# A fused mixer and two feed-forward layers on one core: the opening stretch of the instruction stream put in order by a list scheduler, and two more units' decays made by products

## The chip, the cores and the metric

One core of one Trainium2 chip. The metric is the device time of one execution in microseconds; the median of 3 runs of the kernel before is 615.81 us (613.55 to 616.11).

## The reference

A chunked linear attention with decays, then two feed-forward layers over its output. Inputs x (4 batches, 8 heads, 768 steps, 32 wide), decays a, and B, C (16 states) are 32-bit floats; the weights come as 64-bit floats.

```python
for c in range(nc):                      # chunks of 32 steps
    cum = np.cumsum(la, axis=-1)         # la: log of the decays
    L = np.exp(cum[:, :, :, None] - cum[:, :, None, :]) * causal
    M = np.einsum('bhin,bhjn->bhij', Cc, Bc) * L
    y[:, :, sl] = M @ xc + (Cc @ state) * np.exp(cum)[..., None]
    state = decay_full * state + sum_j(Bc_j * xc_j * decay_from_j)
x = y as (3072 tokens, 256)
h = (x @ w1) * (x @ w2)                  # 256 -> 1024
x2 = (h @ w3) @ w_out                    # 1024 -> 1024 -> 256
h2 = np.maximum(x2 @ w_in, 0.0)          # 256 -> 2048
out = (h2 * h2) @ w_out2                 # 2048 -> 256
```

## The kernel before

The kernel multiplies w3 by w_out once (`wc`, from 16 steps `wc_step` of 8 products each in the trace), so that h @ w3 @ w_out becomes one product with a 1024 x 256 matrix. Every feed-forward product is made three times with operands split in a high and a low part (`mm3`, L99 to L102).

**Weights.** 44 pieces of 128 x 512 double words (0.52 MB each) come through SP's DMA queue into 7 raw buffers (4 `rawe`, 3 `rawl`; `load_next`, L178, issues at L193). A piece is decoded from 64 to 32 bits in `decode1` (ACT L206 and POOL L208, one on each half of a double word) and `decode2` (DVE L221, which joins the halves). The 24 pieces of w1, w2, w_in (`wi`) and the last weight (`wo`) are then split in `decode3` (ACT L231 makes the high part, POOL L232 the low part). The pieces of w3 and the first w_out (`wo1`) go unsplit into `wc`.

**Units.** The attention is cut into 16 units (a batch's half of the sequence, 4 heads, 4 chunks of 96). A unit scans its decays (`u_decay`, DVE L272), weighs B with them (`u_bd`, POOL L287 and L294), makes B times C and the state's gains on PE (`u_cb`, L350; `u_gain`, L305), multiplies the decays in (`u_m`, L363), steps and carries the state (`u_state`, `u_carry`), and multiplies out (`u_y`, L370; `u_x`, `u_xl`). The decays of units 0 and 1 come to the scan by a product of PE that copies a row to all partitions in PSUM (`u_rows`, L259); those of units 2 to 15 are written to DRAM and read back, broadcast to 112 partitions (`load_la`, L139).

**Blocks.** The 3072 tokens go through the feed-forward layers in 7 blocks, 3 of 384 and 4 of 480. A block has 8 steps `ff_a` (products with w1 and w2), each followed by `ff_x2` with wc, and 16 steps `ff_h1`, `ff_h2` and `ff_o`: for 384 tokens 336 products.

**Order.** The order of the instructions of each engine is the order of this program; nothing reorders it. Ahead of block 0 are 29 slots (`n_first`): each runs parts of the decoding of one to three pieces, the `wc_step` that has become possible, and what the tables `first_steps` and `pre` give for units 0 and 1. Then each block has 24 slots, one per step; unit 2 begins 2 slots ahead of block 0, the others at the slots of `BEGIN`, with their 12 parts at the offsets of `unit_steps`. Unit 4 begins at slot 17 of block 0 and ends in block 1. The decoding of wi and wo goes on inside block 0.

The lines that set it:

```python
BEGIN = [None, None, -2, 8, 17, 26, 34, 42, 50, 57, 69, 79, 93, 103, 112, 122]
...
    for i in range(n_first):
        for f in pre.get(i, ()):
            f()
        if i >= LATE:
            decode(first=False)
        for key in [key for key in stage if key[0] == "w3"]:
            wc_step(key[1] % 2, key[1] // 2)
        run_fill()
        for _ in range(1 + (i == 0)):
            decode(second=False)
```

Of the kernel before, what the change touches and what calls it, by code (L numbers as in the profile page):

```python
# [15 lines left out]
T = 96  # L16
# [27 lines left out]
FIRST = 2  # L44
FSTEPS = 8


BEGIN = [None, None, -2, 8, 17, 26, 34, 42, 50, 57, 69, 79, 93, 103, 112, 122]
LATE = 1
# [3 lines left out]
def mixer_kernel(ctx, tc, a, bct, xb, cst, *rest):  # L53
# [61 lines left out]
    def clip_decays():  # L115
# [15 lines left out]
        for i in (0, 32):  # L131
            nc.vector.tensor_copy(sel[i:i + 32, :], cs[i:i + 32, i:i + H])
        z = az.rearrange("(b f g) (h i) -> f b (g h) i", f=2, g=2, i=LH)
        for f in range(2):
            nc.sync.dma_start(out=z[f], in_=t[:, f, :])

    def load_la(u, q):
        t = at.tile([TA, LA], F32, tag="la", name="la")
        q.dma_start(out=t, in_=az[u:u + 1, :].to_broadcast([TA, LA]))  # L139
        raw.setdefault(u, {})["la"] = t  # L140

    def load_bx(u, q):
        t = at.tile([TA, HC * D + HC * N], F32, tag="xa", name="xa")
        q.dma_start(out=t[0:T, :], in_=xb[u])
        for h in range(HG):
            src = bct[u, 0:64, :].rearrange("(n h) (c i) -> h n c i", h=HG, i=T)[h]
            q.dma_start(out=bt[u % 2][32 * h:32 * h + N, :, 0:T], in_=src)
        raw.setdefault(u, {})["xa"] = t

    def load_c(u, q):  # L150
        t = at.tile([128, TB], F32, tag="ct", name="ct", bufs=1)
        for h in range(HG):
            q.dma_start(out=t[32 * h:32 * h + N, :], in_=bct[u, 64:128, :].rearrange("(n h) i -> h n i", h=HG)[h])
        raw.setdefault(u, {})["ct"] = t
# [23 lines left out]
    def load_next():  # L178

        if not loads:  # L180
            return
        key = loads[0]
        for where, n in [("early", NRE)] * (key not in LAST) + [("late", NRL)]:
            if len(held.setdefault(where, [])) < n:
                break
        else:
            return
        loads.pop(0)
        i = min(i for i in range(n) if i not in held[where])
        held[where].append(i)  # L190
        t = (rawe if where == "early" else rawl)[:, i]
        dst = t.rearrange("p (k m) t -> p k (m t)", m=DM) if key[0] in ("wo1", "wo") else t
        nc.sync.dma_start(out=dst, in_=piece_src(key))  # L193
        words[key] = t, where, i
# [8 lines left out]
    def decode1(key):  # L203
        t = words[key][0]
        z = t[:, :, 1].bitcast(F32)
        nc.scalar.activation(z, z, AF.Prelu, scale=2.0 ** -112, alpha=2.0 ** 32)  # L206
        if True:
            nc.gpsimd.tensor_scalar(t[:, :, 0], t[:, :, 0], 0.876 * 2.0 ** -29, 0.49, ALU.mult, ALU.add)  # L208
        else:
            nc.scalar.activation(t[:, :, 0], t[:, :, 0], AF.Copy, bias=0.49, scale=0.876 * 2.0 ** -29)  # L210

    def decode2(key):
        t, where, i = words.pop(key)
        held[where].remove(i)
# [9 lines left out]
    def decode3(key):  # L224
        if key[0] in ("w3", "wo1"):
            return
        if key in (("wo", 0), ("wo", 4)):
            to_wo(key[1] // 4)
        hi, lo = split_to(key)
        v = stage.pop(key).bitcast(F32)  # L230
        nc.scalar.copy(hi, v)  # L231
        nc.gpsimd.tensor_tensor(lo, v, f32(hi), op=ALU.subtract)  # L232

    pend = []
    whole = []

    def decode(first=True, second=True):

        while second and whole:
            decode3(whole.pop(0))  # L240
        if second and pend:
            whole.append(pend.pop(0))
            decode2(whole[-1])
            load_next()
            load_next()
        if first and todo:
            decode1(todo[0])
            pend.append(todo.pop(0))
# [5 lines left out]
    def u_rows(u, h):  # L254

        if h == 0:
            un[u] = dict(raw[u], la=at.tile([TA, LA], F32, tag="la", name="la"))
        r = u % 2 * HG + h
        nc.tensor.matmul(  # L259
            rows[h % 2][0:TA, 0:LH],  # L260
            lhsT=sel[:, r:r + 1].to_broadcast([64, TA]),
            rhs=raw["a"][:, u // 2 % 2, :],
            start=True, stop=True,
        )

# [30 lines left out]
    def u_gain(u):  # L296
# [3 lines left out]
        if "yu" not in d:  # L300
            d["yu"] = ps_yu.tile([128, 512], F32, tag="yu", name="yu")
# [32 lines left out]
    def u_cb(u, hs):  # L334
# [3 lines left out]
        d["ct"] = raw[u]["ct"]  # L338
        for h in hs:
            if h < 2 or len(hs) == 2:  # L340
                d["cb", h] = ps_cb.tile([128, TB], F32, tag="cb", name="cb")
            elif h == 2:
                d["cb", h] = ps_w.tile([128, 512], F32, tag="w", name="cbw")[:, 0:TB]
            else:
                d["yu"] = ps_yu.tile([128, 512], F32, tag="yu", name="yu")
                d["cb", h] = d["yu"][:, 0:TB]
# [9 lines left out]
        if hs[-1] == HG - 1 and u + 1 < NU:  # L356
            load_c(u + 1, nc.sync)
# [36 lines left out]
    def u_xl(u):  # L394
        for lo, src, hi in un.pop(u)["x"]:
            nc.vector.tensor_tensor(lo, src, f32(hi), op=ALU.subtract)

    def u_next(u):

        raw.pop(u)  # L400
        if u + 2 < NU:
            if u + 2 >= FIRST:
                load_la(u + 2, nc.sync)
            load_bx(u + 2, nc.sync)

    def unit_steps(u):
# [42 lines left out]
    def ff_a(f, m):  # L449
        x, n = xt[f], FBS[f]  # L450
        ps = []
        for w in w12:
            p = ps_w.tile([128, 512], F32, tag="w", name="pw")[:, 0:n]
            for k in range(KD):
                mm3(p, [t[:, k, m * 128:(m + 1) * 128] for t in w], [t[:, k, 0:n] for t in x], k == 0, k == KD - 1)
            ps.append(p)
        asb = sb.tile([128, FB], F32, tag="s1", name="asb")[:, 0:n]
        nc.scalar.copy(asb, ps[0])  # L458
        pr = sb.tile([128, FB], F32, tag="s2", name="pr")[:, 0:n]
        nc.vector.tensor_tensor(pr, ps[1], asb, op=ALU.mult)  # L460
        pt[f, m] = [t[:, 0:n] for t in pair("s3", LAG + 1)]
        nc.scalar.copy(pt[f, m][0], pr)  # L462
        return lambda: nc.vector.tensor_tensor(pt[f, m][1], pr, f32(pt[f, m][0]), op=ALU.subtract)  # L463

    def ff_x2(f, m, e):
# [3 lines left out]
        if m == M1 - 1:  # L469
            if e == 0:  # L470
                x2[f] = [t[:, :, 0:FBS[f]] for t in pair("x2", 1, (128, KD, FB))]
            nc.scalar.copy(x2[f][0][:, e, :], acc["x2"][e])  # L472
            nc.vector.tensor_tensor(x2[f][1][:, e, :], acc["x2"][e], f32(x2[f][0][:, e, :]), op=ALU.subtract)
# [7 lines left out]
    def ff_h2(f, m):  # L481
        r = sb.tile([128, FB], F32, tag="s1", name="r")[:, 0:FBS[f]]
        nc.scalar.activation(r, hp.pop(m), AF.Relu)  # L483
        q = sb.tile([128, FB], F32, tag="s2", name="q")[:, 0:FBS[f]]

        (nc.gpsimd if f > 0 else nc.vector).tensor_tensor(q, r, r, op=ALU.mult)  # L486
        qt[f, m] = [t[:, 0:FBS[f]] for t in pair("s3", LAG + 1)]
        nc.scalar.activation(qt[f, m][0], r, AF.Square)  # L488
# [229 lines left out]
```

## Time and profile before

| | us |
|---|---|
| median of 3 runs | 615.81 |
| the profiled execution | 615.05 |
| its span | 613.3 |
| PE, DVE, ACT, POOL busy | 572.3, 317.2, 265.2, 213.4 |

The span runs from the first to the last instruction of the execution; the other 1.8 us lie around it. Busy shares are means over a stretch of opening work and seven blocks, so they are read stage by stage. A group of instructions has its line of the program, engine, operation, output and inputs, and count; in the prediction, L and a number is such a line.

### The profile page before, as it was taken

To read this page: it belongs to the slowest core of one execution; us is meant where nothing else is said; L and a number is where in the kernel's file an instruction comes from. 1 tells how busy PE (TensorE), PEld (TensorE's weight loads), DVE (VectorE), ACT (ScalarE), POOL (GpSimd) and SP (SyncE) were. 2 spreads that over 40 slices of the span, in tenths; PEclk is the share of its full clock that TensorE was granted. 3 is DMA by queue.
4 is the path that set the end of the run, shared out by engine and by line. 5 is a ranking of instruction groups with operands and counts; after the bars stand their busy time and mean duration, and the time that the engine had idled before them with its cause. 6 is when DMAs were issued, how large, how long until landed. Compare 5 with 4: busy or idle time off the path is not lost.

```text
span 613.3 us, 10509 instructions
## 1 busy us (share of the span) xinstructions
PE 572.3 (93%) x4036; PEld 497.6 (81%) x4036; DVE 317.2 (52%) x548; ACT 265.2 (43%) x524; POOL 213.4 (35%) x263
## 2 busy tenths in 40 slices
PE   4986869777999999999999999999999999999997
PEld 2754759566999999998988888888888888888886
DVE  4573565779474765565534635366636352232421
ACT  2334355546344553364323543335434254432543
POOL 3443678675103640153200732107330143300432
PEclk7888798989999999999999999999999999999999
DMA  7997752260211221211210220102110000000000
GB/s 214 301 264 252 272 171 77 92 192 0 79 63 42 77 75 35 73 53 33 73 33 1 79 71 1 40 2 76 49 35 32 1 1 1 1 34 0 1 0 33
DMA packets 20969, 44.86 MB, mean 73 GB/s; under 512 B 7592, under 2 KB 10648, under 8 KB 20920
## 3 DMA queue, kind: packets, MB, share of 16 engines
q1 hardware_dynamic: 20712, 43.93, 23.4%
q8 instruction: 32, 0.52, 0.4%
q10 hardware_dynamic: 208, 0.27, 0.2%
q14 instruction: 17, 0.14, 0.1%
HBM read 40.94 MB, written 3.25 MB: 72 GB/s over the span
## 4 chain that ended last, share of the span: by engine, by line
PE 82%; DVE 5%; POOL 5%; issue 3%; DMA 3%; ACT 1%; ACTq 0%; DVEq 0%; POOLq 0%; SPq 0%
PE pw L102 41%; PE acc L102 31%; PE acc L524 4%; PE yu L370 2%; PE cb L350 2%; DMA cs<-in_cst 1%; DVE la L272 1%; POOL w2l L232 1%; DMA rawe<-in_w3t 1%; PE yu L305 1%; DMA rawl<-in_wo 1%; POOL rawe L208 1%; POOL w1l L232 1%; DVE q L486 1%; DVE s3l L489 1%
## 5 line engine op out<-in xcount | busy, mean ns | idle before, releaser
L486 POOL TENSOR_TENSOR q<-r 128x480 f32<-128x480 f32 (+1 forms) x96 | 103.0, 1076 | 227.0 <-ACT r L483 193.4
L489 DVE TENSOR_TENSOR s3l<-q,s3h 128x480 fp32r<-128x480 f32 (+1 forms) x112 | 74.4, 668 | 116.6 <-POOL q L486 115.5
L102 PE MATMUL acc<-s3h,wo 128*128 128x480 f32 (+1 forms) x448 | 128.5, 368 | 0.0
L483 ACT ACTIVATE r<-pw 128x480 f32<-128x480 f32 (+1 forms) x112 | 59.9, 535 | 120.4 <-PE pw L102 110.7
L102 PEld LDWEIGHTS acc<-s3h,wo 128*128 128x128 f32 x448 | 82.8, 190 | 9.4 <-issue 0.3
L102 PE MATMUL pw<-x2h,wih 128*128 128x480 f32 (+1 forms) x224 | 83.1, 371 | 1.5 <-ACT r L483 0.8
L102 PE MATMUL acc<-s3l,wo 128*128 128x480 f32 (+1 forms) x224 | 82.0, 366 | 2.2 <-DVE s3l L489 2.2
L102 PE MATMUL pw<-x2h,wil 128*128 128x480 f32 (+1 forms) x224 | 81.4, 363 | 0.0
L102 PE MATMUL pw<-x2l,wih 128*128 128x480 f32 (+1 forms) x224 | 79.2, 364 | 0.0
L460 DVE TENSOR_TENSOR pr<-pw,asb 128x480 f32<-128x480 f32 (+1 forms) x56 | 34.4, 614 | 85.3 <-PE pw L102 83.5
L488 ACT ACTIVATE s3h<-r 128x480 fp32r<-128x480 f32 (+1 forms) x112 | 64.0, 571 | 3.5
L462 ACT CAST s3h<-pr 128x480 fp32r<-128x480 f32 (+1 forms) x56 | 31.3, 559 | 78.3 <-DVE pr L460 78.3
L272 DVE TENSOR_TENSOR_SCAN la<-la,cs 112x384 f32<-112x384 f32 x56 | 63.7, 1137 | 0.0
L458 ACT COPY asb<-pw 128x480 f32<-128x480 f32 (+1 forms) x56 | 29.3, 523 | 58.4 <-PE pw L102 58.0
L287 POOL TENSOR_TENSOR bd<-xa,la 96x256 f32<-96x256 f32 x16 | 12.7, 796 | 109.9 <-DVE la L286 47.2
L102 PEld LDWEIGHTS pw<-x2h,wih 128*128 128x128 f32 x224 | 42.4, 189 | 8.9 <-ACT x2h L472 2.7
L524 PE MATMUL acc<-wo1v,ve 128*128 128x256 f32 x128 | 39.1, 469 | 10.5 <-DVE ve L221 10.4
L102 PEld LDWEIGHTS acc<-s3l,wo 128*128 128x128 f32 x224 | 42.5, 190 | 6.9 <-DVE s3l L489 3.1
L102 PEld LDWEIGHTS pw<-x2h,wil 128*128 128x128 f32 x224 | 42.4, 189 | 3.8
L102 PEld LDWEIGHTS pw<-x2l,wih 128*128 128x128 f32 x224 | 42.3, 189 | 3.9
L102 PE MATMUL pw<-xth,w2l 128*128 128x480 f32 (+1 forms) x112 | 41.2, 368 | 3.4 <-POOL w2l L232 3.4
L102 PE MATMUL acc<-s3l,wch 128*128 128x480 f32 (+1 forms) x112 | 41.0, 366 | 2.8 <-DVE s3l L463 2.8
(85 smaller groups left out, 1002.1 us busy)
## 6 DMA issues: line engine op xcount, KB each, us to landing
la<-az SPq DMA_DIRECT2D x14, 679.0 KB, 5.5
rawe<-in_w3t SPq DMA_DIRECT2D x10, 512.0 KB, 6.6
xa<-in_xb SPq DMA_DIRECT2D x16, 288.0 KB, 6.0
rawe<-in_wo SPq DMA_DIRECT2D x6, 512.0 KB, 4.1
rawl<-in_w3t SPq DMA_DIRECT2D x6, 512.0 KB, 7.6
rawl<-in_wo SPq DMA_DIRECT2D x6, 512.0 KB, 4.1
rawl<-in_w_in SPq DMA_DIRECT2D x6, 512.0 KB, 4.1
rawl<-in_w SPq DMA_DIRECT2D x5, 512.0 KB, 5.5
```

The lines of the kernel that those rows point to most:

```text
L102: nc.tensor.matmul(ps, lhsT=w[i == 1], rhs=x[i == 2], start=first and i == 0, stop=last and i == 2)
L232: nc.gpsimd.tensor_tensor(lo, v, f32(hi), op=ALU.subtract)
L272: nc.vector.tensor_tensor_scan(la[:, 0:TB], src[:, 0:TB], cs, 0.0, ALU.mult, ALU.add)
L287: nc.gpsimd.tensor_tensor(bd[u % 2][:, 0:HC * N].rearrange("p (h c n) -> p h c n", h=HG, n=N), d["xa"][0:T, HC * D:].rearrange("p (h c n) ...
L458: nc.scalar.copy(asb, ps[0])
L460: nc.vector.tensor_tensor(pr, ps[1], asb, op=ALU.mult)
L462: nc.scalar.copy(pt[f, m][0], pr)
L483: nc.scalar.activation(r, hp.pop(m), AF.Relu)
L486: (nc.gpsimd if f > 0 else nc.vector).tensor_tensor(q, r, r, op=ALU.mult)
L488: nc.scalar.activation(qt[f, m][0], r, AF.Square)
L489: return lambda: nc.vector.tensor_tensor(qt[f, m][1], q, f32(qt[f, m][0]), op=ALU.subtract)
L524: nc.tensor.matmul(wps[j // 2][:, (j % 2) * DM:(j % 2 + 1) * DM], lhsT=t[:, j * 128:(j + 1) * 128], rhs=wo1v[:, k, :].bitcast(F32), start= ...
```

## The change

It replaces the 29 slots, block 0's loop and the tables of units 0 to 4 by a list of operations with an engine, a cost in us, what they come after, and the buffers they take and free. `Plan.order` goes through them in time and puts, on the engine that can begin first, the operation that can begin first (of those within 0.02 us the one with the longest way to the end, or with a given order for the loads). The instructions are issued in that order. Steps that were one function become several (`ff_a` becomes `a_mm`, `a_copy`, `a_mul`, `a_hi`, `a_lo`; `decode1` to `decode3` become `dec_high`, `dec_low`, `dec_join`, `dec_hi`, `dec_lo`). Units 0 to 3 take their decays by products into one of the three shared PSUM buffers `w`; unit 4 still loads them. Unit 4 is wholly in the list; units 5 and later keep their slots. The order of the pieces is new. From the fifth step on, block 0's products a go into space of `wi` that is not yet written. The loads of B and C of a unit are issued together, and C has two buffers.

```diff
-FIRST = 2
-FSTEPS = 8
-BEGIN = [None, None, -2, 8, 17, 26, 34, 42, 50, 57, 69, 79, 93, 103, 112, 122]
-LATE = 1
+ROWS = 4
+EARLY = 5
+BEGIN = {5: 26, 6: 34, 7: 42, 8: 50, 9: 57, 10: 69, 11: 79, 12: 93, 13: 103, 14: 112, 15: 122}
...
+    pieces = sum(g[:3], []) + w12p[0] + g[3] + w3p[1][:4] + w12p[1] + w3p[1][4:]
     for f in range(4):
+        pieces += [("wi", f), ("wi", 4 + f), ("wo", 2 * f), ("wo", 2 * f + 1)]
...
+    plan = Plan(
+        dict(early=NRE, late=NRL, v=2, w=3, cb=2, s1=2, s2=2, s3=LAG + 1, acc=2, at=2),
+        dict(PE=9.5, DVE=9.5, ACT=7.1, POOL=11.3, SP=0.7),
+    )
...
+        op(("load", key), "SP", 1.78, [], lambda key=key: load_piece(key), [where], order=-20 - i)
+        op(("high", key), "ACT", 0.67, [("load", key)], lambda key=key: dec_high(key))
+        op(("low", key), "POOL", 0.72, [("load", key)], lambda key=key: dec_low(key))
...
+        op(("join", key), "DVE", 0.7, after, lambda key=key: dec_join(key), ["v"] * split, [(where, ("load", key))])
...
+            if key in (("wi", 2), ("wi", 3), ("wi", 6), ("wi", 7)):
+                after += [("x2", M1 - 1, e) for e in range(KD)]
...
+            op(("hi", key), "ACT", 0.56, after, lambda key=key: dec_hi(key))
+            op(("lo", key), "POOL", 1.3, [("hi", key)], lambda key=key: dec_lo(key), frees=[("v", ("join", key))])
...
+        prev = lambda k: [(k, u - 2)] if u >= 2 else []
...
+            op(("bx", u, i), "SP", 0.5 if i == 0 else 0.15, prev("y") + prev("state"), f, order=-20 - (2.5, 8.5)[u] - 0.01 * i if u < 2 else -5 - 0.01 * i)
+        if u < ROWS:
+            for h in range(HG):
+                op(("rows", u, h), "PE", 0.45, prev("y") if h == 0 else [("rows", u, 0)], lambda h=h: u_rows(u, h), ["w"])
+        else:
+            op(("la", u), "SP", 2.4, prev("y") + [("z", 0), ("z", 1)], lambda: load_la(u), order=-4)
...
+        op(("bd", u), "POOL", 1.9, [("lw", u), ("bx", u, 0)] + prev("cb") + prev("state"), lambda: u_bd(u))
...
+    for t, e, eng, k in plan.order():
+        plan.ops[k][3]()
```

## Rows read from the trace of the kernel before

**Rows 1.** The page's 40 slices of the span (15.3 us each), in tenths.
```profile
PE   4986869777999999999999999999999999999997
PEclk7888798989999999999999999999999999999999
DMA  7997752260211221211210220102110000000000
```
**Rows 2.** Busy time by stage: us, engines busy (instructions), granted clock, DMA share, GB/s.
```profile
core 0: us, PE busy (x) PEld busy (x) DVE busy (x) ACT busy (x) POOL busy (x), PEclk, DMA share, GB/s
0.00:9.50 9.50, 4.10 (x12) 1.49 (x12) 2.19 (x10) 3.23 (x4) 1.31 (x13) 0.91 0.80 230
9.50:73.00 63.50, 49.02 (x329) 36.55 (x329) 34.20 (x61) 21.65 (x40) 33.77 (x48) 0.77 0.86 277
73.00:112.00 39.00, 31.58 (x210) 28.87 (x208) 25.36 (x41) 21.46 (x43) 29.41 (x27) 0.91 0.35 115
112.00:160.58 48.58, 39.88 (x303) 36.09 (x303) 40.56 (x62) 27.28 (x59) 27.86 (x25) 0.93 0.35 102
0.00:160.58 160.58, 124.58 (x850) 102.99 (x851) 102.32 (x174) 73.62 (x144) 92.35 (x112) 0.86 0.58 182
160.58:228.04 67.46, 67.42 (x627) 64.74 (x627) 40.40 (x76) 30.32 (x68) 20.62 (x31) 1.00 0.19 55
...
60.00:70.00 10.00, 6.85 (x18) 5.56 (x19) 4.50 (x6) 3.05 (x5) 9.43 (x8) 0.54 1.03 357
```
**Rows 3.** Waits in 0 to 160.6 us: total, times, longest.
```profile
PE acc L524 <- DVE ve L221: 10.4, 4, 7.6
```
**Rows 4.** POOL: durations (ns least/median/most) by line, then two groups of 0 to 160.58 us.
```profile
L208 POOL TENSOR_SCALAR rawl<-rawl x23: 643/835/2481, 16.6 to 139.6; 128x512 uint32<-128x512 uint32 x23
L232 POOL TENSOR_TENSOR wo<-v,wo x8: 1265/1278/3457, 97.2 to 147.3; 128x512 fp32r<-128x512 f32 x8
...
L294 POOL COPY w2s<-la 16x4 f32<-16x4 f32 x20 | 4.3, 215 | 0.9
L287 POOL TENSOR_TENSOR bd<-xa,la 96x256 f32<-96x256 f32 x5 | 4.2, 846 | 13.0 <-PE acc L102 8.4 <-DVE la L274 4.3
```
**Rows 5.** The timeline: start, duration, engine; POOL and DVE.
```profile
11.36 2.59 POOL L208 TENSOR_SCALAR rawe<-rawe 128x512 uint32<-128x512 uint32 x3
...
140.97 1.30 POOL L232 TENSOR_TENSOR wil<-v,wih 128x512 fp32r<-128x512 f32 x1 [0.52 <-ACT wih L231]
140.99 1.68 DVE L489 TENSOR_TENSOR s3l<-q,s3h 128x384 fp32r<-128x384 f32 x1
...
144.48 4.12 POOL L232 TENSOR_TENSOR wo<-v,wo 128x512 fp32r<-128x512 f32 x2 [2.21 <-ACT wo L231]
144.60 0.54 DVE L489 TENSOR_TENSOR s3l<-q,s3h 128x384 fp32r<-128x384 f32 x1
...
145.07 0.55 DVE L486 TENSOR_TENSOR q<-r 128x384 f32<-128x384 f32 x1
145.53 0.68 DVE L221 SCALAR_TENSOR_TENSOR v<-rawl 128x512 uint32<-128x512 uint32 x1
```
**Rows 6.** The scans of line 272 in 0 to 160.58 us (ns least/median/most).
```profile
L272 DVE TENSOR_TENSOR_SCAN la<-la,cs x12: 942/949/2041, 68.2 to 154.3; 112x384 f32<-112x384 f32 x12
L272 DVE TENSOR_TENSOR_SCAN la<-rows,cs x8: 941/950/957, 10.2 to 38.4; 112x384 f32<-112x384 f32 x8
```
**Rows 7.** DMA issues in 0 to 160 us: count, KB each, us to landing.
```profile
la<-az SPq DMA_DIRECT2D x4, 679.0 KB, 6.5
```
**Rows 8.** PE groups in 0 to 160.58 us: the products that copy a row.
```profile
L259 PE MATMUL rows<-al,sel 64*112 64x388 f32 x8 | 4.0, 541 | 8.1 <-DVE sel L132 4.2 <-DVE la L274 4.0
```
**Rows 9.** PE from 160.58 us on: three products in the timeline, a group to 228.04 us.
```profile
160.75 0.33 PE L102 MATMUL pw<-xth,w1h 128*128 128x384 f32 x1
160.93 0.33 PE L102 MATMUL pw<-xth,w1l 128*128 128x384 f32 x1
161.10 0.33 PE L102 MATMUL pw<-xtl,w1h 128*128 128x384 f32 x1
...
L350 PE MATMUL cbw<-ct,bt 16*112 16x96 f32 x24 | 3.1, 266 | 0.0
```

More of the change, by code (lines that the diff above doesn't have):

```diff
@@ L43, with __init__, op, order @@
 LAST = [("wi", 2), ("wi", 6), ("wo", 4), ("wo", 5), ("wi", 3), ("wi", 7), ("wo", 6), ("wo", 7)]
-FIRST = 2
-FSTEPS = 8
-BEGIN = [None, None, -2, 8, 17, 26, 34, 42, 50, 57, 69, 79, 93, 103, 112, 122]
-LATE = 1
+ROWS = 4
+EARLY = 5
+BEGIN = {5: 26, 6: 34, 7: 42, 8: 50, 9: 57, 10: 69, 11: 79, 12: 93, 13: 103, 14: 112, 15: 122}
+class Plan:
+    LAT = 0.2
+    def __init__(self, rings, start):
+        self.ops, self.free, self.taken, self.start = {}, {}, {}, dict(start)
+        self.rings = rings
+    def op(self, name, eng, cost, after, fn, takes=(), frees=(), ready=0.0, order=None):
+        assert name not in self.ops, name
+        self.ops[name] = [eng, cost, list(after), fn, list(takes), ready, order]
+        for ring, who in frees:
+            self.free.setdefault((ring, who), []).append(name)
+    def order(self):
+        ops = self.ops
+        tail = {}
+        users = {}
+        for k, o in ops.items():
+            for d in o[2]:
+                users.setdefault(d, []).append(k)
+        def way(k):
+            if k not in tail:
+                tail[k] = ops[k][1] + max([way(u) for u in users.get(k, ())], default=0.0)
+            return tail[k]
+        for k in ops:
+            way(k)
+        end, left, out = {}, dict(ops), []
+        dmas, wire = [], 0.0
+        while left:
+            best = None
+            for eng in set(o[0] for o in left.values()):
+                can = []
+                for k, o in left.items():
+                    if o[0] != eng or any(d not in end for d in o[2]):
+                        continue
+                    t = max([self.start[eng], o[5]] + [end[d] + self.LAT for d in o[2]])
+                    for ring in o[4]:
+                        n = len(self.taken.get(ring, ())) - self.rings[ring]
+                        if n < 0:
+                            continue
+                        who = self.free.get((ring, self.taken[ring][n]), [])
+                        if any(w not in end for w in who):
+                            t = None
+                            break
+                        t = max([t] + [end[w] + self.LAT for w in who])
+                    if t is not None:
+                        can.append((t, k))
+                if not can:
+                    continue
+                first = min(t for t, _ in can)
+                if eng == "SP" and len(dmas) >= 8:
+                    first = max(first, dmas[-8])
+                near = [(-(o if (o := ops[k][6]) is not None else tail[k]), k, max(t, first)) for t, k in can if t <= first + 0.02]
+                _, k, t = min(near)
+                if best is None or t < best[0]:
+                    best = (t, eng, k)
+            assert best, list(left)[:20]
+            t, eng, k = best
+            o = left.pop(k)
+            self.start[eng] = t + (0.4 if eng == "SP" else o[1])
+            end[k] = self.start[eng]
+            if eng == "SP":
+                wire = max(wire, t + 1.7) + o[1]
+                end[k] = wire + 0.6
+                dmas.append(end[k])
+            for ring in o[4]:
+                self.taken.setdefault(ring, []).append(k)
+            out.append((t, end[k], eng, k))
+        return out
@@ L176, in piece_src, with load_piece @@
         return src[k * 128:(k + 1) * 128, f * PC:(f + 1) * PC, :]
[L178 to L191, printed above, removed]
+    def load_piece(key):
+        where = place(key)
+        n = used.get(where, 0)
+        used[where] = n + 1
+        t = rawe[:, n % NRE] if where == "early" else rawl[:, n % NRL]
         dst = t.rearrange("p (k m) t -> p k (m t)", m=DM) if key[0] in ("wo1", "wo") else t
         nc.sync.dma_start(out=dst, in_=piece_src(key))
-        words[key] = t, where, i
+        words[key] = t
     def split_to(key):
@@ L201, in split_to, with dec_high, dec_low, dec_join @@
         return [x[:, k, f * PC:(f + 1) * PC] for x in {"w1": w12[0], "w2": w12[1], "wi": wi}[nm]]
-    def decode1(key):
-        t = words[key][0]
-        z = t[:, :, 1].bitcast(F32)
+    def dec_high(key):
+        z = words[key][:, :, 1].bitcast(F32)
         nc.scalar.activation(z, z, AF.Prelu, scale=2.0 ** -112, alpha=2.0 ** 32)
[L207 to L214, printed above, removed]
+    def dec_low(key):
+        t = words[key]
+        nc.gpsimd.tensor_scalar(t[:, :, 0], t[:, :, 0], 0.876 * 2.0 ** -29, 0.49, ALU.mult, ALU.add)
+    def dec_join(key):
+        t = words.pop(key)
         if key[0] == "wo1":
@@ L222, in decode2, with dec_hi, dec_lo @@
         stage[key] = v
-    def decode3(key):
-        if key[0] in ("w3", "wo1"):
-            return
+    def dec_hi(key):
         if key in (("wo", 0), ("wo", 4)):
             to_wo(key[1] // 4)
+        nc.scalar.copy(split_to(key)[0], stage[key].bitcast(F32))
+    def dec_lo(key):
         hi, lo = split_to(key)
[L230 to L248, printed above, removed]
+        nc.gpsimd.tensor_tensor(lo, stage.pop(key).bitcast(F32), f32(hi), op=ALU.subtract)
     un = {}
@@ L332, in u_carry, with u_cb @@
             )
-    def u_cb(u, hs):
+    def u_cb(u):
         d = un[u]
[L338 to L346, printed above, removed]
+        hs = range(HG)
+        for h in range(2):
+            d["cb", h] = ps_cb.tile([128, TB], F32, tag="cb", name="cb")
+        d["cb", 2] = ps_w.tile([128, 512], F32, tag="w", name="cbw")[:, 0:TB]
+        d["yu"] = ps_yu.tile([128, 512], F32, tag="yu", name="yu")
+        d["cb", 3] = d["yu"][:, 0:TB]
         for c in range(NCH):
@@ L468, in ff_x2, with x2_hi, x2_lo @@
         mm3(acc["x2"][e], [t[:, m, e * 128:(e + 1) * 128] for t in wc], pt[f, m], m == 0, m == M1 - 1)
[L469 to L473, printed above, removed]
+        if m == M1 - 1 and f > 0:
+            x2_hi(f, e)
+            x2_lo(f, e)
+    def x2_hi(f, e):
+        if e == 0:
+            x2[f] = [t[:, :, 0:FBS[f]] for t in pair("x2", 1, (128, KD, FB))]
+        nc.scalar.copy(x2[f][0][:, e, :], acc["x2"][e])
+    def x2_lo(f, e):
+        nc.vector.tensor_tensor(x2[f][1][:, e, :], acc["x2"][e], f32(x2[f][0][:, e, :]), op=ALU.subtract)
     def ff_h1(f, m, k, which=(0, 1, 2)):
@@ new lines, in mixer_kernel @@
+    for f in range(2):
+        op(("z", f), "SP", 0.4, [], lambda f=f: store_decays(f), ready=10.0, order=0)
+    for i, key in enumerate(pieces):
+        where = place(key)
+        op(("load", key), "SP", 1.78, [], lambda key=key: load_piece(key), [where], order=-20 - i)
+        op(("high", key), "ACT", 0.67, [("load", key)], lambda key=key: dec_high(key))
+        op(("low", key), "POOL", 0.72, [("load", key)], lambda key=key: dec_low(key))
+        split = key[0] not in ("w3", "wo1")
+        after = [("high", key), ("low", key)]
+        if key[0] == "w3":
+            n = [k for k in pieces if k[0] == "w3"].index(key)
+            if n >= NVE:
+                prev = [k for k in pieces if k[0] == "w3"][n - NVE][1]
+                after.append(("wc", prev % 2, prev // 2))
+        op(("join", key), "DVE", 0.7, after, lambda key=key: dec_join(key), ["v"] * split, [(where, ("load", key))])
+        if split:
+            after = [("join", key)]
+            if key in (("wi", 2), ("wi", 3), ("wi", 6), ("wi", 7)):
+                after += [("x2", M1 - 1, e) for e in range(KD)]
+            if key == ("wo", 0):
+                after += [("wc", 1, M1 - 1)]
+            elif key[0] == "wo" and key[1] < 4:
+                after += [("hi", ("wo", 0))]
+            elif key == ("wo", 4):
+                after += [("join", k) for k in pieces if place(k) == "early"]
+            elif key[0] == "wo":
+                after += [("hi", ("wo", 4))]
+            op(("hi", key), "ACT", 0.56, after, lambda key=key: dec_hi(key))
+            op(("lo", key), "POOL", 1.3, [("hi", key)], lambda key=key: dec_lo(key), frees=[("v", ("join", key))])
@@ new lines, in mixer_kernel @@
+    for f in range(2):
+        for k in range(M1):
+            after = [("join", ("w3", 2 * k + f)), ("join", ("wo1", k // 2))] + ([("wc", f, k - 1)] if k else [])
+            op(("wc", f, k), "PE", 1.95, after, lambda f=f, k=k: wc_mm(f, k), ["acc"] * (2 if k == 0 else 0))
+        for q in range(2):
+            op(("wch", f, q), "ACT", 0.6, [("wc", f, M1 - 1)], lambda f=f, q=q: wc_hi(f, q))
+            op(("wcl", f, q), "DVE", 0.7, [("wch", f, q)], lambda f=f, q=q: wc_lo(f, q), frees=[("acc", ("wc", f, 0))])
@@ L631, in ph_a @@
                     ff_x2(f, m - LAG, e)
-            if f == 0 and m % 2 == 0:
-                decode()
         for m in range(M1 - LAG, M1):
@@ L645, in ph_h @@
                     ff_h1(f, m, k)
-            lo = ff_h2(f, m)
-            if f == 0 and m % 4 < 3:
-                decode()
+            h_relu(f, m)
+            h_sq(f, m)
+            h_hi(f, m)
             run_fill()
-            lo()
+            h_lo(f, m)
             if m >= LAG:
@@ L653, in ph_h, with o_tail @@
                     ff_o(f, m - LAG, e)
+        return o_tail(f)
+    def o_tail(f):
         return [lambda m=m: [ff_o(f, m, e) for e in range(KD)] for m in range(M2 - LAG, M2)]
-    while whole:
-        decode3(whole.pop(0))
-    tail = []
-    for f in range(NF):
+    tail = o_tail(0)
+    for f in range(1, NF):
         ph_a(f, tail)
@@ L663, in mixer_kernel @@
         f()
-    assert not fill and not todo and not pend and not whole, (fill, todo, pend)
+    assert not fill, fill
 def kernel(**inputs):
```

295 lines of the change are left out of this document (158 added, 137 removed).

## The prediction

> **What bounds the kernel now.** I read the page's 40 slices first [rows 1]. The PE line is full from the eleventh slice (15.3 us each) on and ragged ahead of it, and the DMA line is busy in the ragged part only. So the kernel has two regimes, and the edit touches the first. The table by stage gives their border [rows 2]: block 1 begins at 160.6 us, PE is busy for 67.42 of the 67.46 us after that, and for 124.58 of the 160.58 us ahead of it. So 36.0 us of the opening stretch are PE idle time, and part of the busy time is slow: the granted clock is 0.77 in 9.5 to 73 us, a mix of the levels 1.2 and 2.4 GHz, and 1.00 in block 1.
>
> The stretch has two halves. In 9.5 to 73 us the DMA share is 0.86 at 277 GB/s [rows 2]: the weights set the pace, and PE's first products of w3 with wo1 wait 10.4 us for the joined words of DVE [rows 3]. From 73 us on the DMA share is 0.35, with PE, DVE, ACT and POOL all partly idle. What then holds them is the decoding of the weights, which goes through ACT, POOL, DVE, ACT and POOL in turn.
>
> POOL and DVE hinder each other there. Alone, POOL's two decoding operations take 0.64 and 1.27 us at the least, but up to 2.5 and 3.5 us [rows 4]. The timeline shows why [rows 5]: L489 on DVE takes 0.54 us at 144.60, but 1.68 us at 140.99, where it ends 0.40 us after the POOL instruction that began 0.02 us before it (140.97 + 1.30). Two POOL splits beside a run of DVE operations took 4.12 us instead of 2.5. The scans show the same by where their input lies [rows 6]: 12 with both inputs in SBUF take 942 to 2041 ns, 8 that read the row from PSUM take 941 to 957 ns. The Trainium skill's page "SBUF — State Buffer", section "SBUF: two separate sides", says that a DVE operation with two SBUF inputs and a GpSimd operation that reads SBUF hold a shared port pair one at a time, for the whole instruction; the trace agrees with it at 140.99 us.
>
> **The change, part by part.**
>
> *Decays of units 2 and 3.* Two loads of 679 KB go (0.68 MB at 277 GB/s is 2.5 us of the queue each, 4.9 us in the half that the DMA bounds) [rows 2, 7]. PE gets 8 more products, 8 x 0.541 = 4.3 us [rows 8]. DVE's 8 scans now read PSUM, 8 x 0.95 us, outside the pair; 8 small products of the row ends come instead of two longer ones, under 1 us. Instead of a round trip through DRAM the scans wait for a PE product and one of three PSUM buffers. Those are shared with the other products: a scan that is late holds PE back, and whatever stands behind it in PE's order.
>
> *Order.* Instead of slots written by hand, every instruction of the stretch (44 pieces of weights, units 0 to 4, block 0) is put out in the order that a list scheduler finds. I bound that order by what each engine must do, and take nothing from the scheduler's own times.
>
> PE. Busy time times granted clock is 4.10 x 0.91 + 49.02 x 0.77 + 31.58 x 0.91 + 39.88 x 0.93 = 107.3 us at full clock [rows 2]; less the warm-up's 3.7, plus 4.3 for the rows and 2.9 for unit 4 (below), that is 110.8 us after 9.5 us. At a full clock without idle time the stretch would end at 120 us, at the 0.86 of before at 138 us.
>
> The pair. I sum the POOL operations and the DVE operations with two SBUF inputs at their undisturbed times. POOL: 44 first decodes x 0.64, 24 splits x 1.27, and 4.3 + 4.2 for the units' bd and w2s = 67.2 us [rows 4]. DVE: 44 joins x 0.68, 12 scans x 0.945, 16 x 0.55 for L486, 24 x 0.54 for L489 and L463 = 63 us [rows 5, 6]. Undisturbed DVE operations begin 0.47 us apart where each shows 0.55 [rows 5], so some 0.08 us of each of about 96 is not holding anything: less 8. That is 122 us of work before, in 149 us (POOL's first decode begins at 11.4 us [rows 5]): 82% used. After it is 8 x 0.95 = 7.6 us less: 114.6 us. Used fully it ends at 126 us, at 82% at 151 us. I take 90%, because the hand-written slots are what leaves gaps after 73 us, and a greedy order fills these, but the half that waits for DMA stays: 11.4 + 127 = 138.5 us. PE's end for a clock of 0.92 with 9 us of idle time is 9.5 + 120.4 + 9 = 139 us, the same place. So the stretch shrinks by 160.6 - 138.5 = 22.1 us.
>
> DMA is no longer the last bound: 44 pieces of 0.52 MB and five units of 0.49 MB are 25.6 MB, at 277 GB/s 92 us, before 100 us with the start.
>
> *Unit 4 ends in the first stretch.* Before, its products run inside block 1, which therefore holds three units (24 of L350's products into cbw, 8 a unit) [rows 9]. Block 1 has 336 products of its own, 0.175 us apart [rows 9], 58.8 us; the rest of its 67.46 us [rows 2] is 8.7 us, 2.9 us a unit. Block 1 loses one: -2.9 us. Its cost in the first stretch is in the sums above.
>
> *Other edits.* Half of block 0's products go into space of wi that isn't yet written, so they need not wait for wc; the splits of four wi pieces then wait for x2 (queued behind them: POOL's last splits). The order of the pieces puts w1 and w2 ahead of half of w3. I cost both inside the 90%. From block 1 on the steps keep their slots; 0, bounded by +-1 us. Loads of C get a second buffer and go with the unit's others: SP issues the same 9 per unit, none more; 0.
>
> **The sum.** Against the profiled execution (615.05 us, span 613.3): 615.05 - 22.1 - 2.9 = 590.0 us. The median of the runs, 615.81, is 0.1% off, which I neglect.
>
> **The rivals.**
>
> A, the forecast: the end of the stretch at 131 to 146 us, so 582.5 to 597.5 us. Chance 0.55.
>
> B, better: gaps close, the pair is fully used, and PE keeps a clock of 0.95 (9.5 + 116.6 = 126 us): 615.05 - 34.6 - 2.9 = 577.5 us. For it speaks that PE now has units, w3 and a's products to choose from while it waits. Against it: each piece passes four operations on three engines. Chance 0.17.
>
> C, less: the pair stays at 82%, end at 151 us, 615.05 - 9.6 - 2.9 = 602.5 us. For it: the scheduler's costs are undisturbed times (44 x 0.72 + 24 x 1.3 + 5 x 1.9 = 72 us of POOL), where POOL showed 92.35 us [rows 2]; an order made for an engine 20 us faster waits in the wrong places. Chance 0.15.
>
> D, no gain: SP's order. The loads of units 2 to 4 stand ahead of the pieces and wait there for y of the unit two before; every piece behind waits too. If each of the three waits held SP's queue for 8.3 us, the 25 us would be gone: 615 us. Against it: 7 raw buffers run ahead. Chance 0.05.
>
> E, slower: the clock. PE's products of the units are short and wait for DVE and ACT; a greedy order strews them among w3's products, and PE's clock may stay low. In 60 to 70 us before, it was 0.54 [rows 2], after PE's longest wait for the joined words [rows 3]. With 20 us of idle time left, the stretch with unit 4 is no shorter than before (163.5 us) when 9.5 + 20 + 110.8/c = 163.5, at a clock c of 0.83; at 0.70 it ends at 188 us and the kernel takes 615.05 + 27.2 - 2.9 = 639 us. Against it: less idle time and a higher clock go together in [rows 2]. Chance 0.08. The Trainium skill's page "TensorE: Matmul & The Clock Gate", section "HAM oscillation — how this bites in real kernels", says that waits between bursts of products bring the half clock back; the 0.54 agrees.
>
> **The numbers.** The likeliest is A, 590 us. Nearly all of A, most of B and the half of C lie in 574 to 605 us. A measurement of this kernel can tell a difference of about 0.5% (3 us) from none. Faster by more: 0.55 + 0.17 + 0.15 = 0.87. Same: 0.05. Slower: 0.08.
>
> **What would show it.** Right: 16 scans from rows and 4 from la; block 1's first product near 138 us; block 1 some 3 us shorter, later blocks the same; a DMA share near 0.9 until 90 us, and PE's granted clock at 0.9 or more from 20 us on. In the half after x2, POOL and DVE should take turns without gaps. Wrong: a first product of block 1 after 150 us with POOL idle (C), DMA idle before 70 us with SP waiting for a unit's y (D), or a clock under 0.8 with PE busy (E).

## The result and the profile after

The changed kernel takes 594.5 us (median of 4 runs, 594.08 to 596.04), the kernel before 614.68 us beside it; the ratio is 0.9678 (95% interval 0.9642 to 0.9714). The forecast was 590.0 us, range 574 to 605. The profiled execution took 594.08 us, with a span of 592.3 us.

The page's slices of the changed kernel (14.8 us each), to be held against [rows 1]:

```profile
PE   5979898889999999999999999999999999999997
PEclk7889798999999999999999999999999999999999
DMA  6878954620003122022002020020300000010000
```

PE is full from the tenth slice on; the ragged part ends sooner, and nothing behind it has changed its look.

The table by stage of the changed kernel, cut where x2 of block 0 is done (102.6 us), where block 1 begins (142.53 us), and where it ends (columns as in [rows 2]):

```profile
0.00:102.60 102.60, 83.23 (x682) 66.15 (x683) 78.73 (x140) 51.50 (x97) 66.94 (x98) 0.89 0.73 239
102.60:142.53 39.93, 35.68 (x273) 32.67 (x273) 28.82 (x47) 24.30 (x51) 16.90 (x15) 0.98 0.37 115
...
0.00:142.53 142.53, 118.91 (x954) 98.83 (x955) 107.55 (x187) 75.79 (x148) 83.84 (x112) 0.92 0.63 204
142.53:207.09 64.56, 64.52 (x529) 62.63 (x529) 37.97 (x69) 29.13 (x63) 20.31 (x30) 1.00 0.12 37
...
9.50:142.53 133.03, 113.86 (x941) 96.57 (x941) 105.33 (x177) 72.55 (x144) 81.94 (x97) 0.91 0.62 202
```

The same table of the kernel before, cut where its x2 is done:

```profile
0.00:111.55 111.55, 84.25 (x547) 66.74 (x548) 61.75 (x112) 45.89 (x85) 64.49 (x87) 0.83 0.68 218
111.55:160.58 49.03, 40.33 (x305) 36.26 (x304) 40.56 (x62) 27.73 (x59) 27.86 (x25) 0.93 0.34 101
```

The 21 us of span come from three places. The way to x2 is 9.0 us shorter (111.55 to 102.60), the rest of block 0 is 9.1 us shorter (49.03 to 39.93), and block 1 is 2.9 us shorter (67.46 in [rows 2], 64.56 now). What follows lasts as long as before: 613.3 - 228.0 and 592.3 - 207.1 are both 385.2 us. Ahead of x2 the new order lets DVE do 78.73 us of work in 102.6 us, where 61.75 us in 111.55 us were done before. Of that work, 11.7 us are missing from the second part: DVE had been busy there for 40.56 of 49.03 us and now is for 28.82 of 39.93. PE, busy for 35.68 us, now nearly sets the length of this part. In the whole stretch PE is idle for 23.6 us (142.53 - 118.91), before 36.0 us, and its granted clock is 0.92, before 0.86.

The scans of the changed kernel in 0 to 140 us (ns least/median/most), as in [rows 6]:

```profile
L329 DVE TENSOR_TENSOR_SCAN la<-rows,cs x16: 940/949/956, 9.5 to 71.6; 112x384 f32<-112x384 f32 x16
L329 DVE TENSOR_TENSOR_SCAN la<-la,cs x4: 944/1426/1594, 87.7 to 96.2; 112x384 f32<-112x384 f32 x4
```

Its waits up to 145 us, of PE and of SP's queue (total, times, longest):

```profile
PE acc L586 <- DVE ve L293: 2.7, 2, 1.7
...
SPq L267 <- DVE v L293: 21.4, 8, 4.5
SPq L267 <- DVE ve L293: 9.6, 7, 2.1
SPq L217 <- PE yu L423: 7.7, 2, 6.8
```

Sixteen scans read PSUM and none of them is stretched; the four that read SBUF still are. PE's wait of [rows 3] for the joined words of w3 fell from 10.4 to 2.7 us. SP waits 31.0 us for DVE's joins, that is for a raw buffer to come free. In the kernel before it was 60.1 us, up to 160.58 us:

```profile
SPq L193 <- DVE v L221: 52.3, 14, 12.0
...
SPq L193 <- DVE ve L221: 7.8, 7, 2.2
```

ACT, which begins the decoding, in turn waits 28.5 us for pieces to land in the changed kernel (9.5 to 145 us): by these sums the decoding and the loads hold each other about equally. SP's wait for a unit's y, the place of rival D, is 7.7 us.

### The profile page after: what moved, and what is told of

The parts are those of the page before. It is cut to its first block, busy times and chain, and to the rows that moved or that the text cites. A ratio compares the mean times of both kernels' runs of the same rounds, so it can differ in the third digit from the quotient of the medians.

```text
span 592.3 us, 10511 instructions
## 1 busy us (share of the span) xinstructions
PE 563.9 (95%) x4044; PEld 491.5 (83%) x4044; DVE 319.9 (54%) x554; ACT 266.3 (45%) x524; POOL 204.9 (35%) x263
## 4 chain that ended last, share of the span: by engine, by line
PE 78%; DMA 9%; DVE 6%; POOL 2%; issue 2%; ACT 2%; SPq 1%; DVEq 0%; POOLq 0%; ACTq 0%
PE pw L178 41%; PE acc L178 32%; DMA rawl<-in_w3t 3%; DMA rawl<-in_wo 2%; PE yu L423 2%; PE cb L405 2%; DMA xa<-in_xb 1%; DVE la L329 1%; DVE v L293 1%; DMA rawe<-in_w3t 1%; DVE ve L293 1%; DMA rawl<-in_w_in 1%; POOL rawl L283 1%; PE yu L363 1%; ACT xa L387 1%
## 5 line engine op out<-in xcount | busy, mean ns | idle before, releaser
L178 PE MATMUL acc<-s3h,wo 128*128 128x480 f32 (+1 forms) x448 | 127.2, 365 | 1.3 <-ACT s3h L548 1.3
L178 PEld LDWEIGHTS acc<-s3h,wo 128*128 128x128 f32 x448 | 81.9, 188 | 10.7 <-ACT s3h L548 1.6
L508 ACT CAST s3h<-pr 128x480 fp32r<-128x480 f32 (+1 forms) x52 | 29.3, 563 | 69.0 <-DVE pr L497 69.0
L329 DVE TENSOR_TENSOR_SCAN la<-la,cs 112x384 f32<-112x384 f32 x48 | 54.1, 1127 | 0.0
L347 POOL TENSOR_TENSOR bd<-xa,la 96x256 f32<-96x256 f32 x16 | 14.5, 904 | 106.8 <-DVE la L341 83.4
L178 PE MATMUL pw<-xth,w1h 128*128 128x480 f32 (+1 forms) x112 | 41.4, 370 | 1.0 <-DVE la L331 0.5
L178 PE MATMUL pw<-xth,w2h 128*128 128x480 f32 (+1 forms) x112 | 42.2, 377 | 0.0
L511 DVE TENSOR_TENSOR s3l<-pr,s3h 128x480 fp32r<-128x480 f32 (+1 forms) x52 | 33.3, 640 | 15.3 <-ACT s3h L508 15.1
```

The costliest lines, as they stand in the source:

```text
L178: nc.tensor.matmul(ps, lhsT=w[i == 1], rhs=x[i == 2], start=first and i == 0, stop=last and i == 2)
L347: nc.gpsimd.tensor_tensor(bd[u % 2][:, 0:HC * N].rearrange("p (h c n) -> p h c n", h=HG, n=N), d["xa"][0:T, HC * D:].rearrange("p (h c n) ...
L508: nc.scalar.copy(pt[f, m][0], ab[m])
L511: nc.vector.tensor_tensor(pt[f, m][1], ab.pop(m), f32(pt[f, m][0]), op=ALU.subtract)
```

## The experiments

Theory ahead of the runs: the pair of POOL and DVE sets the length of the stretch, so that work taken from it shortens the time nearly one to one. Rivals: the loads, the chain of a piece's decoding, PE's clock. Each kernel is the changed one with one edit (in one case two together); the diffs show the main lines. The changed kernel unaltered was timed a second time, beside the last three.

**How far two measurements agree**

> The changed kernel once more, unaltered, to be compared with the three others on one chip: 594 to 596 us. How far it lies from 594.5 us shows what a difference of these runs is worth.

595.2 us, ratio 0.9694 (0.9668 to 0.9719). So 0.9678 and 0.9694 are one kernel. Half the width of its intervals is 0.36% and 0.25%, so an edit within some 0.4% (2.5 us) of it isn't told apart from it by one measurement.

**The decays of two units loaded again**

```diff
-ROWS = 4
+ROWS = 2
```

> The changed kernel (594.5 us) with the decays of units 2 and 3 loaded again, the scheduler kept. Theory (the pair of POOL and DVE sets the opening stretch): 8 scans of 0.95 us return to operations with two SBUF inputs, so 7.6 us more of pair work at some 90% use, less the 3 us of PE products that go: block 1 begins 3 to 8 us later, 598 to 602 us. Rival (the scans are off the path, only the order counts): 594 to 595.5 us.

601.2 us, 0.9786 (0.9763 to 0.9809): 6.7 us of the 20 us are the decays' part (6.0 us against the second measurement), and no interval of the changed kernel reaches it. Block 1 begins at 149.37 us, 6.8 us later, 5.1 of which are there at x2 (107.7 us). The theory's number came in, but the edit brings back two things, stretched scans and loads. Two runs bring back one each.

```diff
+    def u_row_copy(u, h):
+        nc.scalar.copy(un[u]["la"][:, h * LH:(h + 1) * LH], rows.pop((u, h))[0:TA, 0:LH])
...
```

> The changed kernel with the rows of units 2 and 3 still made by products, but copied by ACT from PSUM into SBUF, so that their 8 scans have two SBUF inputs again, without a load. Theory (the loaded decays cost 6.7 us because their scans take the pair): most of it comes back, 597.5 to 601 us. Rival (they cost because 1.4 MB more are loaded and waited for): 594 to 596 us.

```diff
...
+            op(("spare", u, i), "SP", 1.2, prev("y") + [("z", 0), ("z", 1)],
+               lambda i=i: nc.sync.dma_start(out=spare, in_=az[u:u + 1, 600 * i:600 * i + 600].to_broadcast([128, 600])), order=-4 - 2 * i)
```

> The changed kernel with four added loads of 307 KB (1.23 MB, broadcast, into a tile that nobody reads) issued with the loads of units 2 and 3. Theory (pair): the loads are not waited for and cost 0 to 1.5 us, 594 to 596 us. Rival (DMA bandwidth and SP's queue make the loaded decays dear): 4 to 7 us more, 598.5 to 601.5 us.

The copied rows gave 597.0 us, 0.9712 (0.9695 to 0.9729), the spare loads 597.6 us, 0.9721 (0.9690 to 0.9753). Each lies between its theory and its rival, 2 to 3 us above the changed kernel's median (its ratio 0.2 to 0.4% above), with an interval that overlaps both of the changed kernel's. In their traces block 1 begins at 143.86 and 145.87 us (142.53 and 141.60 us in the changed kernel's two). The scans of the copied rows were stretched again:

```profile
L329 DVE TENSOR_TENSOR_SCAN la<-la,cs x12: 942/1100/2034, 33.6 to 88.8; 112x384 f32<-112x384 f32 x12
L329 DVE TENSOR_TENSOR_SCAN la<-rows,cs x8: 941/947/957, 9.5 to 23.4; 112x384 f32<-112x384 f32 x8
```

Both point to a cost, neither is clear of the noise, and the copied rows also put 8 copies of 0.49 us on ACT. So that the decays cost 6 to 7 us is shown; how that divides between the pair and the loads is not.

**Work taken from the pair**

Squares of block 0 from PSUM:

```diff
-        (nc.gpsimd if f > 0 else nc.vector).tensor_tensor(q, hr[m], hr[m], op=ALU.mult)
...
+            nc.vector.scalar_tensor_tensor(q, p, 0.0, hr[m], ALU.max, ALU.mult)
```

> The changed kernel with block 0's 16 squares on DVE made from the product in PSUM and r (max with 0, times r) in place of r times r, so that they have one SBUF input. Theory (the pair): 16 x 0.47 = 7.5 us of pair work go, half of them in the last 12 us where PE is full anyway: 3 to 5 us less, 590 to 592 us. Rival (the chain of one piece's decoding and the loads set the pace): no change, 594 to 595 us, or slower by up to 2 us because a PSUM buffer is held until DVE has read it.

Low words on ACT, for wi and wo, then for every second piece (there the condition is `pieces.index(key) % 2 == 1`):

```diff
+        if key[0] in ("wi", "wo"):
+            nc.scalar.activation(t[:, :, 0], t[:, :, 0], AF.Copy, bias=0.49, scale=0.876 * 2.0 ** -29)
...
```

> The changed kernel with the first decoding step of the low words of the last 16 pieces (wi and wo) on ACT and not on POOL. Theory (the pair): 16 x 0.64 = 10 us of pair work go, ACT takes 11 us more and has 0.55 busy there: 4 to 8 us less, 587 to 591 us. Rival (ACT's place in the chain of each piece sets the pace): ACT's two decoding steps come one after the other, 0.7 us later each piece: 595 to 600 us.

> The changed kernel with the first decoding step of the low words of every second piece (22 of 44, the early ones too) on ACT and not on POOL. Theory (the pair holds the time up to x2, 9.5 to 104 us, not the time after, where PE is full): x2 ends 4 to 7 us sooner and the time falls by as much, 587.5 to 590.5 us. Rival (the loads set the pace up to x2): 593.5 to 596 us.

Low parts on DVE:

```diff
+        eng = nc.vector if key[0] in ("wi", "wo") else nc.gpsimd
+        eng.tensor_tensor(lo, stage.pop(key).bitcast(F32), f32(hi), op=ALU.subtract)
...
```

> The changed kernel with the low part of the split of the last 16 pieces (wi and wo) on DVE, where it should take about 0.7 us, and not on POOL (1.27 us). Theory (the pair): 16 x (1.27 - 0.6) = 10.7 us of pair work go: 2 to 6 us less, 588.5 to 592.5 us. Rival (DVE itself is the bound, 107.55 of 142.5 us busy): 9.6 us more on DVE, 595 to 602 us.

Half the low words and the squares together:

> Both reliefs of the pair at once: the low words of every second piece on ACT, and block 0's squares from PSUM; 22 x 0.64 + 16 x 0.47 = 21.6 us less pair work. Theory (the pair holds the time up to x2; after x2 the eight last pieces, which must wait for it, hold it): 590 to 593 us, no more than the low words alone gave. Rival (the pair holds both): 585 to 589 us.

| run | off the pair, us | median us | ratio (interval) | block 1 begins, us |
|---|---|---|---|---|
| squares | 7.5 | 594.0 | 0.9663 (0.9633 to 0.9692) | 142.68 |
| low words, wi and wo | 10 | 592.6 | 0.9640 (0.9613 to 0.9666) | 138.40 |
| low parts on DVE | 10.7 | 592.9 | 0.9658 (0.9609 to 0.9707) | 139.93 |
| low words, half | 14 | 592.4 | 0.9643 (0.9617 to 0.9668) | 140.63 |
| half, and squares | 21.6 | 591.0 | 0.9639 (0.9608 to 0.9670) | 139.42 |

All five lie below the changed kernel, by 0.5 to 4 us, where one to one would have been 7 to 21 us; none is clear of both measurements of the changed kernel. Only the last came in within its theory's range; the squares came in at their rival's, the other three above their theory's and short of their rival's. The theory falls in its one-to-one form. That the pair is one limit of several that lie close together fits this, but is not shown: the edits also put work on ACT or DVE, or hold a PSUM buffer longer, and what that cost was not separated.

The table by stage of the kernel with half the low words on ACT, cut at its x2 and its block 1, and then the same of the changed kernel's second profile:

```profile
0.00:97.40 97.40, 83.15 (x651) 65.48 (x652) 74.01 (x131) 60.45 (x115) 51.38 (x74) 0.89 0.74 241
97.40:140.63 43.23, 38.55 (x305) 35.80 (x304) 34.06 (x57) 26.36 (x56) 18.18 (x16) 0.92 0.45 130
...
0.00:99.90 99.90, 85.08 (x682) 66.83 (x683) 77.98 (x140) 51.10 (x98) 66.53 (x99) 0.88 0.76 247
99.90:141.60 41.70, 37.68 (x273) 34.57 (x273) 28.90 (x47) 24.42 (x51) 16.67 (x14) 0.93 0.35 106
```

With half the low words on ACT, x2 is done at 97.4 us, 5.2 us sooner than in the first profile of the changed kernel and 2.5 us sooner than in its second. But the rest of block 0 takes 43.23 us, 3.3 us more than in the first and 1.5 us more than in the second. PE's idle time in that rest is 4.7 us, in the first profile 4.3 us; what grew is its busy time, 38.55 against 35.68 us, at a granted clock of 0.92 against 0.98. Four stretches show where:

```profile
98.50:101.00 2.50, 0.01 (x2) 0.01 (x1) 2.50 (x5) 0.50 (x1) 0.00 (x0) 1.00 0.69 240
...
102.20:105.80 3.60, 3.60 (x40) 2.93 (x38) 2.61 (x7) 2.94 (x7) 2.71 (x3) 0.53 0.01 5
...
114.30:115.90 1.60, 0.02 (x1) 0.02 (x1) 1.60 (x3) 0.51 (x1) 0.51 (x1) 1.00 0.09 26
115.90:119.40 3.50, 3.50 (x11) 3.50 (x12) 3.22 (x8) 1.30 (x5) 1.34 (x1) 0.51 0.80 223
```

PE stands for 2.5 us until DVE makes the low part of x2, which comes behind three scans of unit 4 there, and for 1.6 us until DVE makes a low part of block 0's squares. Soon after each wait it runs some 3.5 us at about half the clock. So in this trace the earlier x2 was lost again in waits for DVE and in the slow clock behind them. The changed kernel's second profile, with no edit at all, has the same pattern more weakly: an earlier x2, then a longer rest at a lower clock.

What stands ahead of the second wait is partly the pair. POOL's line in the timeline of that run, and DVE's beside it:

```profile
104.75 0.68 DVE L296 SCALAR_TENSOR_TENSOR v<-rawl 128x512 uint32<-128x512 uint32 x1
...
104.91 3.48 POOL L350 TENSOR_TENSOR bd<-xa,la 96x256 f32<-96x256 f32 x1 [0.81 <-DVE la L344]
...
105.35 0.55 DVE L554 TENSOR_TENSOR s3l<-q,s3h 128x384 fp32r<-128x384 f32 x1
105.82 0.55 DVE L547 TENSOR_TENSOR q<-r 128x384 f32<-128x384 f32 x1
106.29 0.68 DVE L296 SCALAR_TENSOR_TENSOR v<-rawl 128x512 uint32<-128x512 uint32 x1
106.89 0.55 DVE L554 TENSOR_TENSOR s3l<-q,s3h 128x384 fp32r<-128x384 f32 x1
107.36 0.55 DVE L547 TENSOR_TENSOR q<-r 128x384 f32<-128x384 f32 x1
107.83 0.55 DVE L453 TENSOR_TENSOR xtl<-yu,xth 128x384 fp32r<-128x384 f32 x1
```

That POOL instruction, 622 ns at its shortest in that run, stood 3.48 us while DVE put six operations with two SBUF inputs one after the other. It ends at 108.39 us, 0.56 us after one with a PSUM input has begun (107.83). Behind it on POOL wait unit 4's other steps and the next split, at 109.64 us, and behind that split DVE's next join, at 110.98 us, ahead of the low part that PE waits for.

**The order's other parts**

```diff
-    pieces = sum(g[:3], []) + w12p[0] + g[3] + w3p[1][:4] + w12p[1] + w3p[1][4:]
+    pieces = sum(g, []) + w3p[1][:4] + w12p[0] + w3p[1][4:] + w12p[1]
```

> The changed kernel with the pieces of the weights in the order of before (all of the first half of w3, then four pieces of the second half, w1 and w2's first four, the last of w3, w1 and w2's last four). Theory (the order of the pieces is a small part of the scheduler's gain, since the same 28 pieces must be decoded ahead of x2): 594 to 597 us. Rival (the early w1 and w2 pieces are what fills PE's wait for w3): block 0's products start later and PE is idle again, 599 to 606 us.

594.9 us, 0.9690 (0.9657 to 0.9723): as the theory has it, and by that interval the order of the pieces brings at most some 4 us of the gain.

```diff
-        op(("low", key), "POOL", 0.72, [("load", key)], lambda key=key: dec_low(key))
+        op(("low", key), "POOL", 0.85, [("load", key)], lambda key=key: dec_low(key))
...
-            op(("lo", key), "POOL", 1.3, [("hi", key)], lambda key=key: dec_lo(key), frees=[("v", ("join", key))])
+            op(("lo", key), "POOL", 1.45, [("hi", key)], lambda key=key: dec_lo(key), frees=[("v", ("join", key))])
```

> The changed kernel with the scheduler's costs of six operations set to the means of the changed kernel's profile (0.85 and 1.45 us on POOL, 0.82, 0.85, 0.70 and 0.72 us on DVE) in place of undisturbed ones. Theory (the order is robust, since each engine takes what is ready): 593 to 596.5 us. Rival C of the prediction (an order made for undisturbed engines waits in the wrong places): 588 to 592 us.

597.5 us, 0.9732 (0.9701 to 0.9764), 2.4 us above the changed kernel timed beside it, with overlapping intervals, and above both ranges. Costs nearer to the truth did not make a better order; rival C's reason finds no support.

```diff
-    for _ in range(12):
+    for _ in range(30):
         nc.tensor.matmul(warm[:, 0:480], lhsT=wt[:, 0:128], rhs=wt, start=True, stop=True)
```

> The changed kernel with 30 products ahead of the first row and not 12, so that PE is not idle before 9.5 us. Theory (PE's clock at the start is no limit, since w3's pieces come at the pace of the loads and the decoding): 593 to 596 us, though the granted clock from 10 to 20 us rises from 0.57. Rival (the slow clock of the first 30 us delays everything behind it): 589 to 592 us.

592.5 us, 0.9662 (0.9635 to 0.9688), against 595.2 us of the changed kernel beside it; between theory and rival, and the intervals overlap. The clock of the slice from 10 to 20 us rose as meant, from 0.51 in the changed kernel's second profile (first line) to 0.69 (second), but x2 was done at 102.7 us and not sooner. The profiled execution was the slowest of the five (595.74 us, the others 592.0 to 592.7), so its trace does not show how the others were faster. Inconclusive.

```profile
10.00:20.00 10.00, 7.30 (x14) 4.28 (x15) 9.80 (x19) 2.02 (x3) 5.47 (x11) 0.51 0.85 263
...
10.00:20.00 10.00, 6.13 (x16) 3.71 (x15) 8.97 (x18) 2.59 (x4) 5.59 (x14) 0.69 0.73 239
```

The fastest version is the one with half of the low words on ACT and the squares from PSUM, 591.0 us (0.9639); the changed kernel timed beside it had 595.2 us (0.9694). The two intervals just touch, so that it is faster is likely and not certain.

## Why the prediction was right

- *Where the gain lies.* Right: all of it is in the opening stretch and in unit 4's move; from block 2 on nothing changed (385.2 us in both).
- *Unit 4.* Right: block 1 went from 67.46 to 64.56 us, 2.9 us as forecast, and holds 16 products into `cbw` where it had 24, two units in place of three.

```profile
L405 PE MATMUL cbw<-ct,bt 16*112 16x96 f32 x16 | 2.0, 266 | 0.0
```

- *The end of the stretch.* Forecast 138.5 us, measured 142.53 (141.60 in the second profile): the 4 us between 590.0 and 594.1 are this term. In PE's sum two errors partly cancel. The work was put too high: after 9.5 us PE is busy 113.86 us at a clock of 0.91, where 120.4 us at 0.92 were forecast. That is 103.6 us at full clock, as much as before without the warm-up (107.3 - 3.7), although 7.2 us had been added for the rows and unit 4; what made up for them is not shown. The idle time was put too low: 133.03 - 113.86 = 19.2 us in place of 9 us.
- *The pair at 90%.* Here a step failed. Its 114.6 us in the 131 us from 11.4 to 142.5 us would be 87%, close to the figure taken, but the 90% was chosen, not worked out, and the pair does not set the end: 7.5 to 21.6 us less of it gave 0.5 to 4 us. That the end came out within 4 us is in this term luck. Two sums that end at the same place were read as a confirmation; the runs confirm neither as the bound.
- *The signs.* The scans (16 from rows, 4 from la), block 1's length and the later blocks came as said. Three signs did not. The DMA share was 0.73 up to x2, not near 0.9. PE's clock fell below 0.9 again after 20 us, to 0.83 in 30 to 40 us and to 0.82 and 0.84 from 60 to 80 us. And in the half after x2 POOL and DVE do not take turns without gaps: POOL is busy for 16.90 of 39.93 us and has nothing more to do from 129.2 us on, while PE is full from 130 us to block 1. The last 12 us are PE's alone, which the pair's sum could not show:

```profile
127.86 1.29 POOL L303 TENSOR_TENSOR wo<-v,wo 128x512 fp32r<-128x512 f32 x1 [1.91 <-ACT wo L299]
...
30.00:40.00 10.00, 6.57 (x77) 4.44 (x75) 6.24 (x12) 5.98 (x12) 7.25 (x12) 0.83 0.77 265
...
130.00:140.00 10.00, 10.00 (x59) 10.00 (x58) 5.05 (x10) 4.07 (x8) 0.00 (x0) 1.00 0.00 1
```

- *The decays.* Scans from PSUM aren't stretched and two loads go, as forecast. In the pair's sum they are 7.6 us; undoing them cost 6.0 to 6.7 us, but for which of the two reasons is open. The remaining 13 us of the 20 are, by difference, the scheduler's order and unit 4's place; what unit 4 costs in the opening stretch was not separated. Which of the order's moves brings the 10 us beyond block 1's 2.9 stays open: the order of the pieces brings little of it, costs nearer to the disturbed ones bring nothing, and the use of wi's space for block 0's products was not tried by itself.
- *The rivals.* D: SP's wait for a unit's y came to 7.7 us, 6.8 of them at one load; what it cost was not tried, but the gain is there. E: the clock rose with PE's use, 0.86 to 0.92. C's time would have been 602.5 us; POOL did the same 112 operations in 83.84 us of busy time where it took 92.35, so it was disturbed less, not more.

## What to carry to other kernels

Where engines wait on each other in turn, a scheduler fed with measured durations can find time that hand-placed slots lose: work that needs no late operand moves forward, and the part behind shrinks to its fullest engine. When several sums of work end within a few us of each other, expect a cut in one to return a fraction (here some sixth to a quarter, within the noise), and look for what gives the rest back. Where DVE and POOL are both busy, an operand left in PSUM can keep a DVE operation at its undisturbed length: 940 to 956 ns for these scans, against up to 1594 ns from SBUF in the same kernel.

## What was not expected

The changed kernel's two profiles, of the same instructions, differ early: x2 was done at 102.6 and 99.9 us, block 1 began at 142.53 and 141.60 us.

PE's clock can fall long after the start. In the kernel with the low words of wi and wo on ACT, block 1 began at 138.4 us, 4.1 us sooner than in the changed kernel, but the span was only 0.9 us shorter. Block 2 had taken 72.00 us, in the changed kernel 68.73 us. Ten-us slices of that run; then of the changed kernel, with its wait in them; then, of the kernel with the longer warm-up, its wait, the slice around it and the two slowest us:

```profile
245.00:255.00 10.00, 8.60 (x99) 7.66 (x97) 7.05 (x13) 4.82 (x12) 6.28 (x9) 0.97 0.45 120
255.00:265.00 10.00, 10.00 (x72) 9.92 (x72) 3.79 (x10) 2.26 (x5) 1.66 (x2) 0.69 0.01 2
...
249.00:259.00 10.00, 8.88 (x133) 7.96 (x131) 7.22 (x13) 4.92 (x12) 4.87 (x9) 1.00 0.41 120
257.64 0.30 PE L405 MATMUL yu<-ct,bt 16*112 16x96 f32 x1 [1.12 <-issue]
259.00:269.00 10.00, 10.00 (x60) 10.00 (x58) 4.16 (x11) 5.23 (x12) 2.94 (x4) 1.00 0.01 2
...
257.92 0.30 PE L405 MATMUL yu<-ct,bt 16*112 16x96 f32 x1 [1.13 <-issue]
255.00:265.00 10.00, 8.87 (x97) 8.35 (x96) 4.20 (x8) 2.92 (x7) 3.13 (x4) 0.83 0.25 68
261.00:263.00 2.00, 2.00 (x8) 2.00 (x7) 0.00 (x0) 0.00 (x0) 0.00 (x0) 0.50 0.00 0
```

In the first, after a slice with 1.4 us of idle time, PE ran 10 us at a granted clock of 0.69, a mix of 1.2 and 2.4 GHz. The changed kernel had 1.1 us of idle time in the same place (8.88 us busy of 10) and kept 1.00 behind it. The longer idle time need not be the reason: in the third run the wait was 1.13 us, in the changed kernel 1.12 us, at the same products (L405), and behind it the clock fell to 0.50 in 261 to 263 us. So the same gap can cost nothing in one execution and, as in the first run, some 3 us in another; that is as much as most of these edits.
